# The first token tile in two halves on two DMA queues, with the bias rows moved behind weight tile 4

## The chip, the cores and the metric

The kernel runs on one core of one Trainium2 chip. The metric is device microseconds (us) of one execution. Five engines matter here: TensorE (PE in the profile; its weight loads are PEld), VectorE (DVE), ScalarE (ACT), GpSimd (POOL) and SyncE (SP). SP and ScalarE issue the DMA transfers; 16 DMA engines move the bytes. In the profile, SPq and ACTq are the issuing instructions of SP and ScalarE. Queue q1 carries what SP issues; q10 carries what ScalarE issues (its 0.33 MB are w1's first columns, b1 and one later store of 256 KB).

## What is computed

x is [2048 tokens, 512 features], bf16. Two branches are mixed by a gate per token:

```python
g = sigmoid((x * gate_w).sum(-1, keepdims=True))
a = A_ref(x, wqkv, wo)          # linear attention, 32 heads of 16
h = layernorm(x)                # over the features of a token
u = gelu(einsum("bsd,sf->bdf", h, w1) + b1)     # mixes over the tokens, F = 1792
b = transpose(einsum("bdf,fs->bds", u, w2) + b2)
out = g * a + (1 - g) * b
```

What the change touches is the start of the second branch: the layer norm of x, and the product of w1 [2048 tokens, 1792] with it, which sums over the tokens.

## The kernel before

The tokens come in 16 tiles of 128 (`NT`), one token in each partition. x tile t is `xr[:, t, :]` (128 KB), its normalised form `xh[:, t, :]`. The rows of w1 that belong to token tile t are tile t of w1. Its first 1024 columns (`FA`, eight blocks of 128) are in `w1A[:, t, :]` (256 KB), the rest in `w1B`, loaded later.

**Order of the loads.** Every DMA is issued by the helper `load` (the issue is line 124), by SP unless ScalarE is named, and `pin` keeps the order in which the program lists the instructions on an engine. ScalarE issues three loads first: the 14 rows of b1 into `b_rows` (line 134, 3.5 KB), then the first 128 columns of w1's tiles 0 and 1 (lines 135 and 136, 32 KB each). Then it loads its table and takes a dummy square root (line 137). SP issues x tile 0 (line 139), x tile 1, the other 896 columns of w1's tile 0 (line 141, 224 KB), and then, from line 142 on, one tile of x and one of w1 in turn; of w1's tile 1 it loads the other 896 columns (line 146). Behind w1's tile 4, it loads the 16 rows of b2 into `b_rows` (line 150). Behind the last tile come gate_w, wk, x transposed, and the other weights. `b_rows` is set to zero by VectorE first (line 114), and the loads into it wait for that. Up to eight transfers are under way at a time: each issue waits until the transfer eight earlier in the common list of SP and ScalarE has landed.

**Layer norm.** VectorE takes the statistics of a tile (`ln_bn`, line 197; tile 0, and 4 and up, in one instruction, tiles 1 to 3 in two of 256 features), combines them (`ln_aggr`, line 200), ScalarE takes the square root (`sd`, line 202), and VectorE the reciprocal (line 208) and the normalised tile (`ln_apply`, line 210). The first half of tile t's statistics stands ahead of the normalisation of tile t-1 on VectorE. At t = 8 VectorE turns `b_rows` into columns (line 232).

**First product.** TensorE starts with 18 matmuls on a constant (`warm_ps`). Then, for each of the first 12 token tiles, it does eight matmuls (`accA`, all issued by the helper in line 74), one for each block of 128 columns of w1A: weights w1A, moving operand xh (128x512). The last four tiles go block by block, and each finished block goes to ScalarE (`gelu`). The keys (`kacc`), `Gps`, the other blocks (`accB`), the queries (`qacc`) and the second product (`yps`) follow. The only waits between the loads and TensorE's first matmuls are thus: x tile 0 to xh tile 0, w1's 128 columns for the first weights, w1's other 896 columns for the next seven, and so on for tile 1.

Of the kernel before, what the change touches and what calls it, by code (L numbers as in the profile page):

```python
# [15 lines left out]
def kernel(  # L16
# [13 lines left out]
    nc = tc.nc  # L30
    P = nc.NUM_PARTITIONS
# [11 lines left out]
    NF = F // P  # L43
# [7 lines left out]
    x_view = X.rearrange("(t p) d -> p t d", p=P)  # L51
# [4 lines left out]
    b1_view = B_b1.rearrange("(f p) -> f p", p=P)  # L56
# [9 lines left out]
    def ptile(shape, dt, name):  # L66
        return persist.tile(shape, dt, name=name, tag=name)
# [9 lines left out]
    xr = ptile([P, NT, D], BF16, "xr")  # L77
# [17 lines left out]
    b_rows = ptile([32, P], BF16, "b_rows")  # L95
# [27 lines left out]
    def load(o, i, eng=None, **kw):  # L123
        pin((eng or nc.sync).dma_start(out=o, in_=i, **kw))  # L124

    def load_x(t0, t1):
        load(xr[:, t0:t1, :], x_view[:, t0:t1, :])

    def load_w1a(t):
        load(w1A[:, t, :], w1_view[:, t, 0:FA])  # L130


    tbl = work.tile([P, 1], FP32, name="tbl", tag="tbl", bufs=2)
    load(b_rows[0:NF, :], b1_view, nc.scalar)
    load(w1A[:, 0, 0:P], w1_view[:, 0, 0:P], nc.scalar)
    load(w1A[:, 1, 0:P], w1_view[:, 1, 0:P], nc.scalar)
    pin(nc.scalar.activation(out=tbl[:], in_=eps_t[:], func=ACT.Sqrt))

    load_x(0, 1)
    load_x(1, 2)  # L140
    load(w1A[:, 0, P:FA], w1_view[:, 0, P:FA])
    for t in range(1, NT):
        if t + 1 < NT:
            load_x(t + 1, t + 2)
        if t == 1:
            load(w1A[:, 1, P:FA], w1_view[:, 1, P:FA])
        else:
            load_w1a(t)
        if t == 4:
            load(b_rows[NF : NF + NT, :], b2_view)  # L150
    load(gw_b[:], gw_row_view.to_broadcast([P, D]))
    load(wk_sb[:], wqkv_view[:, :, D : 2 * D])
# [440 lines left out]
```

## Time and profile before

| what | value |
|---|---|
| median of 3 runs | 162.82 us (162.81 to 162.83) |
| span of the profiled execution, first to last instruction | 161.6 us |
| median less span | 1.2 us |
| TensorE busy | 157.1 us, 97% of the span |
| VectorE / ScalarE busy | 118.7 us (73%) / 53.0 us (33%) |
| mean granted TensorE clock | 0.998 |
| bytes moved | 28.33 MB, 175 GB/s over the span |

The profile shows one execution. A line of a timeline begins with the start and the duration in us; at its end, in brackets, stand the engine's idle time before it and what ended that. In tables of issues the last number is the time from an issue's start to its landing, so that issue plus that time is when the data is there. The profiled execution has no time of its own beside its span; the runs without a profile are 1.2 us above it.

### The profile page before, as it was taken

To read this page: it belongs to the slowest core of one execution; us is meant where nothing else is said; L and a number is where in the kernel's file an instruction comes from. 1 tells how busy PE (TensorE), PEld (TensorE's weight loads), DVE (VectorE), ACT (ScalarE), POOL (GpSimd) and SP (SyncE) were. 2 spreads that over 40 slices of the span, in tenths; PEclk is the share of its full clock that TensorE was granted. 3 is DMA by queue.
4 is the path that set the end of the run, shared out by engine and by line. 5 is a ranking of instruction groups with operands and counts; after the bars stand their busy time and mean duration, and the time that the engine had idled before them with its cause. 6 is when DMAs were issued, how large, how long until landed. Compare 5 with 4: busy or idle time off the path is not lost.

```text
span 161.6 us, 2275 instructions
## 1 busy us (share of the span) xinstructions
PE 157.1 (97%) x820; PEld 72.9 (45%) x820; DVE 118.7 (73%) x279; ACT 53.0 (33%) x89; POOL 1.2 (1%) x8
## 2 busy tenths in 40 slices
PE   7899999999999999999999999999999999999993
PEld 5344444444444444444444444444444444444452
DVE  2799998959998998799895999999999980000002
ACT  3122226895243221435225970000008300550050
POOL 2000000000000000000000000000000000000000
PEclk9999999999999999999999999999999999999999
DMA  4999998444699540229953007826535925824421
GB/s 140 271 320 353 364 300 144 101 103 106 159 394 390 149 129 0 87 50 310 402 200 67 0 32 230 322 65 143 186 89 136 353 70 143 265 63 105 143 97 32
DMA packets 36966, 28.33 MB, mean 175 GB/s; under 512 B 20572, under 2 KB 31452, under 8 KB 36956
## 3 DMA queue, kind: packets, MB, share of 16 engines
q1 hardware_dynamic: 36368, 27.87, 57.0%
q10 hardware_dynamic: 588, 0.33, 0.7%
q8 instruction: 6, 0.10, 0.3%
q14 instruction: 4, 0.03, 0.1%
HBM read 19.28 MB, written 4.46 MB: 147 GB/s over the span
## 4 chain that ended last, share of the span: by engine, by line
PE 94%; DMA 3%; SPq 1%; DVE 0%; issue 0%; DVEq 0%
PE yps L74 39%; PE accA L74 16%; PE accB L74 13%; PE qacc L74 9%; PE Gps L74 9%; PE kacc L74 9%; DMA w1A<-in_B_w_dram 3%; SPq L124 1%; PE kvps L74 0%; DVE ot L537 0%; PE w2ps L74 0%; DVEq L537 0%
## 5 line engine op out<-in xcount | busy, mean ns | idle before, releaser
L74 PE MATMUL yps<-uT,w2h 128*128 128x512 bf16 (+2 forms) x238 | 49.2, 366 | 0.0
L74 PEld LDWEIGHTS <-w2h 128*128 128x128 bf16 x238 | 22.8, 98 | 25.9
L74 PE MATMUL accA<-xh,w1A 128*128 128x512 bf16 x128 | 28.0, 379 | 0.8 <-DVE xh L210 0.5
L530 ACT ACTIVATE ot<-yps,c,c 128x512 bf16<-128x512 f32 x15 | 11.6, 777 | 46.9 <-PE yps L74 35.5
L74 PE MATMUL accB<-xh,w1B 128*128 128x512 bf16 x96 | 21.5, 379 | 0.0
L537 DVE TENSOR_SCALAR ot<-yps,c,c 128x384 bf16<-128x384 f32 (+1 forms) x2 | 1.1, 545 | 25.5 <-PE yps L74 25.5
L74 PEld LDWEIGHTS <-w1A 128*128 128x128 bf16 x128 | 12.5, 98 | 16.1 <-DMA w1A<-in_B_w_dram 1.4
L74 PEld LDWEIGHTS <-xT 128*128 128x128 bf16 x128 | 12.4, 98 | 14.9 <-issue 0.2
L74 PE MATMUL kacc<-wk_sb,xT 128*128 128x512 bf16 x64 | 15.8, 379 | 0.0
L74 PE MATMUL Gps<-pk,xr 128*128 128x512 bf16 x64 | 15.8, 379 | 0.0
L74 PE MATMUL yps<-W2sb,pqT 128*128 128x512 bf16 (+2 forms) x68 | 14.6, 366 | 0.0
L74 PEld LDWEIGHTS <-w1B 128*128 128x128 bf16 x96 | 9.4, 98 | 11.3
L74 PE MATMUL qacc<-wq_sb,xT 128*128 128x512 bf16 x64 | 14.5, 379 | 0.0
L286 ACT ACTIVATE e<-qacc 128x512 bf16<-128x512 f32 x16 | 9.6, 597 | 12.2 <-DVE kvbdT L434 4.6
L286 ACT ACTIVATE e<-kacc 128x512 bf16<-128x512 f32 x16 | 9.2, 598 | 12.7 <-DVE pk L293 6.8
L197 DVE BATCH_NORM_STATS2 stats<-xr 128x6 f32<-128x512 bf16 (+1 forms) x19 | 11.1, 586 | 2.7 <-DMA xr<-in_A_x_dram 2.7
L288 DVE TENSOR_SCALAR e<-e 128x512 bf16<-128x512 bf16 x32 | 9.2, 288 | 4.6 <-ACT e L286 4.3
L406 DVE SCALAR_TENSOR_TENSOR pq<-pq,odds,rd 128x512 bf16<-128x512 bf16 x16 | 12.0, 752 | 0.6
L402 DVE TENSOR_REDUCE den<-prod 128x32 f32<-128x544 f32 x16 | 11.5, 720 | 0.6
L293 DVE SCALAR_TENSOR_TENSOR pk<-kacc,e 128x512 bf16<-128x512 f32 x16 | 11.1, 692 | 1.0
L293 DVE SCALAR_TENSOR_TENSOR pq<-qacc,e 128x512 bf16<-128x512 f32 x16 | 11.1, 692 | 0.6
L245 DVE CUSTOM_DVE_ANT_0 junk<-xr,gw_b 128x512 bf16<-128x512 bf16 x16 | 11.0, 689 | 0.4
(52 smaller groups left out, 95.0 us busy)
## 6 DMA issues: line engine op xcount, KB each, us to landing
w2h<-in_B_w_dram SPq DMA_DIRECT2D x3, 1792.0 KB, 7.5
w1A<-in_B_w_dram SPq DMA_DIRECT2D x14, 256.0 KB, 4.7
w1B<-in_B_w_dram SPq DMA_DIRECT2D x4, 768.0 KB, 6.2
xr<-in_A_x_dram SPq DMA_DIRECT2D x16, 128.0 KB, 4.1
q_dram<-pq SPq DMA_DIRECT2D x16, 128.0 KB, 3.7
out_dram<-ot SPq DMA_DIRECT2D x15, 128.0 KB, 1.8
w2h<-in_B_w_dram SPq DMA_DIRECT2D x1, 1280.0 KB, 6.5
wk_sb<-in_A_wqkv_dram SPq DMA_DIRECT2D x1, 512.0 KB, 6.5
```

The costliest lines, as they stand in the source:

```text
L74: nc.tensor.matmul(o, lhsT=lhsT, rhs=rhs, start=start, stop=stop, **kw)
L124: pin((eng or nc.sync).dma_start(out=o, in_=i, **kw))
L197: pin(nc.vector.bn_stats(out=stats[t][:, h, :], in_=xr[:, t, d0:d1]))
L245: nc.vector.tensor_tensor_reduce(out=junk[:], in0=xr[:, t, :], in1=gw_b[:], scale=1.0, scalar=0.0, op0=ALU.mult, op1=ALU.add, accum_out=gp ...
L286: pin(nc.scalar.activation(out=e[:], in_=acc[:], func=ACT.Exp))
L288: nc.vector.tensor_scalar(out=e[:], in0=e[:], scalar1=1.0, scalar2=PHI_EPS, op0=ALU.min, op1=ALU.add)
L293: nc.vector.scalar_tensor_tensor(out=o, in0=acc[:], scalar=0.0, in1=e[:], op0=ALU.max, op1=ALU.add)
L402: pin(nc.vector.tensor_reduce(out=den[:], in_=prod[:], op=ALU.add, axis=AX.X))
L406: nc.vector.scalar_tensor_tensor(out=heads, in0=heads, scalar=odds[:, t : t + 1], in1=rd[:].unsqueeze(2).to_broadcast([P, NH, HEAD]), op0= ...
L530: nc.scalar.activation(out=ot[:, d0:d1], in_=yps[:, d0:d1], func=ACT.Identity, scale=c1[:, t : t + 1], bias=c2[:, t : t + 1],)
L537: nc.vector.tensor_scalar(out=ot[:, d0:d1], in0=yps[:, d0:d1], scalar1=c1[:, t : t + 1], scalar2=c2[:, t : t + 1], op0=ALU.mult, op1=ALU.add,)
```

## The change

x tile 0 is loaded in two halves of 64 tokens (64 KB each): tokens 64 to 127 on ScalarE's queue, as its first instruction, in the place of b1's rows; tokens 0 to 63 on SP's, in the place of the whole tile. w1's first 128 columns of tiles 0 and 1 stay behind it on ScalarE's queue. b1's 14 rows are now issued by SP, behind w1's tile 4 and ahead of b2's rows. SP has one issue more than before, ScalarE as many as before. The instructions of TensorE, VectorE and GpSimd and their order are the same; the statistics of tile 0 wait for two transfers instead of one, and the turning of `b_rows` waits for two.

```diff
     tbl = work.tile([P, 1], FP32, name="tbl", tag="tbl", bufs=2)
-    load(b_rows[0:NF, :], b1_view, nc.scalar)
+    HP = P // 2
+    load(xr[HP:P, 0, :], x_view[HP:P, 0, :], nc.scalar)
     load(w1A[:, 0, 0:P], w1_view[:, 0, 0:P], nc.scalar)
     load(w1A[:, 1, 0:P], w1_view[:, 1, 0:P], nc.scalar)
     pin(nc.scalar.activation(out=tbl[:], in_=eps_t[:], func=ACT.Sqrt))
 
-    load_x(0, 1)
+    load(xr[0:HP, 0, :], x_view[0:HP, 0, :])
     load_x(1, 2)
     load(w1A[:, 0, P:FA], w1_view[:, 0, P:FA])
     for t in range(1, NT):
...
         if t == 4:
+            load(b_rows[0:NF, :], b1_view)
             load(b_rows[NF : NF + NT, :], b2_view)
```

## Prediction

> **What bounds the kernel now.** I read the chain that ended last first, on the page:
>
> ```profile
> PE yps L74 39%; PE accA L74 16%; PE accB L74 13%; PE qacc L74 9%; PE Gps L74 9%; PE kacc L74 9%; DMA w1A<-in_B_w_dram 3%; SPq L124 1%; PE kvps L74 0%; DVE ot L537 0%; PE w2ps L74 0%; DVEq L537 0%
> ```
>
> TensorE makes up 94% of it, and the only transfer in it is of w1A, with 3%. The same view, cut to the first 25 us and in order of time, says where:
>
> ```profile
> 2.20 0.43 SPq L124
> 2.63 0.04 issue
> 2.67 4.65 DMA w1A<-in_B_w_dram
> 7.32 0.04 issue
> 7.37 17.66 PE accA L74 x81
> ```
>
> From 7.37 us TensorE runs without a break (81 matmuls in 17.66 us, 218 ns each). What starts that run is the SP transfer issued at 2.67, the last 896 columns of w1's tile 1; I call it W1 (and W0 the same part of tile 0). The waits of TensorE over the whole run agree: no wait for an input of over 0.1 us stands behind 7.37 except one of 0.4 for DVE, in its weight loads, which run ahead of the matmuls. So the change, which ends within the first loads, can move the end only as far as it moves 7.37. The timeline of the first 8 us shows what lies ahead of it:
>
> ```profile
> 0.80 0.87 SPq L124 DMA_DIRECT2D xr<-in_A_x_dram  x2
> ...
> 0.87 0.11 DVE L114 MEMSET b_rows<- 32x64 uint32 x1 [0.87 <-PEq L577]
> ...
> 1.02 0.63 ACTq L124 DMA_DIRECT2D b_rows<-in_B_b_dram  x1
> ...
> 1.68 0.86 ACTq L124 DMA_DIRECT2D w1A<-in_B_w_dram  x2
> ...
> 2.58 1.28 ACT L137 ACT_TABLE_LOAD   x1 [2.58 <-issue]
> ...
> 2.92 0.69 DVE L197 BATCH_NORM_STATS2 stats<-xr 128x6 f32<-128x512 bf16 x1 [1.93 <-DMA xr<-in_A_x_dram]
> ...
> 4.95 2.10 PE L74 MATMUL accA<-xh,w1A 128*128 128x512 bf16 x9 [0.50 <-DVE xh L210]
> ...
> 7.37 6.87 PE L74 MATMUL accA<-xh,w1A 128*128 128x512 bf16 x31 [0.31 <-DMA w1A<-in_B_w_dram]
> ```
>
> The reader should see two gaps of TensorE: 0.50 us before its first matmul on data, at 4.95, and 0.31 us before 7.37. The first nine matmuls (eight of token tile 0, one of tile 1) stand between them. **The second gap swallows the first**: if the nine start earlier and W1 lands as now, the second gap only grows. The issue table cut to each issue gives landings: x tile 0 at 0.80 + 2.1 = 2.90, tile 1 at 3.36, w1's first 128 columns of tile 0 at 1.68 + 3.1 = 4.78, W0 at 1.72 + 3.3 = 5.02, x tile 2 at 5.4, W1 at 2.67 + 4.7 = 7.37, x tile 3 at 3.15 + 4.6 = 7.75. Engine use by stretch (columns: window, its length, busy time and count of five engines, granted clock, DMA share, GB/s):
>
> ```profile
> 1.80:2.20 0.40, 0.40 (x4) 0.28 (x2) 0.00 (x0) 0.00 (x0) 0.05 (x1) 1.00 0.66 159
> 2.20:2.60 0.40, 0.40 (x4) 0.28 (x3) 0.00 (x0) 0.03 (x1) 0.00 (x0) 1.00 0.95 309
> ...
> 4.40:5.60 1.20, 0.70 (x5) 0.39 (x4) 1.13 (x5) 0.09 (x1) 0.00 (x0) 1.00 0.83 142
> 5.60:7.00 1.40, 1.40 (x7) 0.49 (x5) 1.33 (x5) 0.21 (x1) 0.00 (x0) 1.00 0.91 291
> ```
>
> The DMA engines start slowly (159 GB/s), then 309, and sag to 142 GB/s while W1 is due. W1 is no matter of its issue: it waits behind 608 KB on SP's queue.
>
> **The change part by part.**
>
> *ScalarE's queue.* b1's 14 rows leave it (1.02 to 1.65, after DVE's memset of b_rows that ended at 0.98), and x's lower 64 tokens come instead, with no wait: start 0.80 like SP's, for 0.40 (SP's first issue) to 0.63 (the row it replaces). The two w1 issues then start at 1.25 to 1.48 instead of 1.68, the Sqrt table load at 2.15 to 2.38 instead of 2.58. I take 0.3 earlier. So w1's 128 columns land at about 4.5 (4.78 now).
>
> *x tile 0.* Each half is 64 KB. How long a half takes isn't in the trace; the nearest rows are the stores at the kernel's end, 128 KB in 1.8 us and 32 KB in 1.4, which give 0.27 us for 64 KB. Bounds: the halves land 0.27 earlier, or, if ScalarE's issue needs 0.63 and its half lands no sooner after it, 0.23 later. I take 0.2 earlier. The statistics need both halves. Further, sd started at 3.98 though its input ended at 3.65 + 0.18 = 3.83, because the table load and the dummy Sqrt ran until then; that 0.12 goes as well (a usual gap there is 0.03). First matmul: 4.95 - 0.2 - 0.12 = 4.63. By itself this is **worth nothing at the end**: the nine matmuls need 9 x 0.22 = 2.0 us and would wait at 6.6 instead of 7.05 for W1 at 7.37.
>
> *SP's queue ahead of W1.* Its number of issues is the same and an issue takes 0.40 to 0.43 whatever its size here (16 rows of b2 took 0.36), so W1 is issued at most 0.05 earlier. But 64 KB less lie ahead of W1 on that queue. Between x tile 0's landing (2.90) and W1's (7.37), it delivered tile 1, W0, tile 2 and W1, 704 KB in 4.47 us: 6.35 ns a KB, so 64 KB are 0.41 us. At the pace of the window 7 to 8 us (370 GB/s) they would be 0.18. They must go by the other queue, though. Room for them is in the slow start: 159 GB/s against 309 in the next 0.4 us is 60 KB not moved, just as ScalarE's half is due: SP's first bytes move at 1.8, 1.0 us behind its first issue, and ScalarE's half is issued as early. I take 0.4 for that reason, as W1's lateness was built up in the slow stretches, and keep 0 and 0.77 as ends. 0.77 is what remains if W1 stops mattering: matmuls that run on from 4.63 reach the tenth at 6.6.
>
> *What is late next.* Tile 2's normalised tokens (DVE, 8.28 + 0.41 = 8.69) are needed at 7.37 + 7 x 0.218 = 8.90: only 0.21 to spare. They wait for x tile 3 (DVE takes tile 3's first half before it finishes tile 2), which lands at 7.75 right behind W1 on the same queue. If W1 comes earlier, tile 3 should; if it doesn't, the gain ends at 0.21. Each later tile is needed 8 x 0.218 = 1.74 later: tile 3 has 10.64 - 10.34 = 0.30 to spare, tile 4 0.87, tile 6 2.0.
>
> *b1 on SP's queue behind tile 4.* One more issue of 0.36, and one more place in the row of eight transfers that may be under way: tile 6 of x was released at 7.34 by W1's landing; now b2 takes that place and tile 6 waits for tile 3's landing, 7.75. The transfers behind come about 0.5 later. Cover: x tile 6 lands at 10.7, then 11.2, and its statistics start at 11.53; w1's tile 5 lands at 7.75 + 3.9 = 11.65, then 12.2, and is needed at 14.13. Without that cover it would cost 0.5. The bias transposes on DVE wait for b1 and b2 at 15.1, long after. Cost: nothing. DVE and TensorE instructions are the same, in the same order.
>
> **Sum.** The profiled execution spans 161.6 us; the median of the runs is 162.82, so about 1.2 lie outside the span, which the change doesn't touch. 161.6 - 0.4 = 161.2, or **162.42** by the median.
>
> The Trainium skill speaks against the change (DMA: Bandwidth & Descriptors, "Issuing engines are not separate DMA queues"): transfers started by SP and ScalarE run on the same 16 DMA engines and interleave, and a second issuing engine saves only issue time. By that rule 64 KB moved to the other queue delay W1 as before, and the time stays at about 162.8. The trace agrees in that both queues move packets in the same stretch (2.6 to 5 us: SP's take 85.4% of the 16 engines' time, ScalarE's 12.6%); that the start leaves 60 KB of room is why I don't follow it all the way.
>
> **The rivals.**
> 1. *Hidden anyway.* The DMA engines are the limit, not the queue, and W1 lands at 7.37 within 0.2. For: 0.82 to 0.95 busy from 2.2 on, and the same bytes in all. Against: the weak start. Time 162.8. (This is where the rule just named leads.)
> 2. *Tile 3 becomes the limit.* W1 lands 0.4 earlier, x tile 3 doesn't, and TensorE stops at token tile 2. Gain 0.21: 162.61. For: slack of only 0.21. Against: both are on one queue.
> 3. *Slower: ScalarE's queue pushes W1 back.* It now has 128 KB instead of 67, and 64 KB of it come ahead of w1's columns; served in turn with SP's, they reach into the stretch of 142 GB/s, where 64 KB cost 0.46: 163.28. It decides once W1 lands later than 7.70. For: that stretch is there and not explained by bytes. Against: ScalarE's issues start earlier.
>
> **How the numbers follow.** 0.2% is 0.33 us, about what a measurement of this kernel can tell from no change. Forecast (gain of 0.33 to 0.77): 0.45. Rival 2: 0.12, rival 1: 0.21, both within 0.2%: 0.33. Rival 3: 0.22. The range goes from the full 0.77 (162.05; rounded to 162.1) to rival 3 (163.28; rounded to 163.2): about 0.02 and 0.1 lie outside.
>
> **What would show it.** W1's landing near 6.97 and the unbroken run from there; first matmul at 4.6 to 4.7 with the gap before the run still open; statistics of tile 0 at 2.7; the table load near 2.3; x tile 6 issued behind tile 3's landing, without a wait on TensorE. I am wrong if W1 still lands at 7.3 or later, if tile 2's normalised tokens end last, or if any wait of TensorE appears behind 9 us.

## The result and the profile after

The changed kernel is slower: ratio 1.0036 to the kernel before, 95% interval 1.0023 to 1.0049, or about 0.6 us. Its median is 163.62 us (163.16 to 164.82, 13 runs) beside 162.87 (162.8 to 163.56, 13 runs) on the same chip. The prediction was 162.42, a gain of 0.4.

The profiled executions tell less than the runs: spans of 161.8 and 161.6. Each later run came with its span, and time less span is 1.7 to 1.8 us throughout, for both kernels, so the 161.6 of the first page belongs to an execution of about 163.3 us, not to the median of 162.82. A second profile of the kernel before has 161.4. Single executions of one kernel spread by about 1 us here, and the traces below show what varies; verdicts rest on ratios of many runs. A run more than 1.5% above the fastest of its kernel is left out of a ratio, which here is one run alone, of 165.82 us.

The chain of the page after:

```profile
PE yps L74 38%; PE accA L74 17%; PE accB L74 13%; PE kacc L74 9%; PE qacc L74 9%; PE Gps L74 8%; DMA xr<-in_A_x_dram 2%; DVE stats L199 0%; PE kvps L74 0%; DVE xh L212 0%; DVE ot L539 0%; PE w2ps L74 0%; ACT sd L204 0%; DVE mv L202 0%; DVE rstd L210 0%
```

The one transfer in the chain is now of x, not of w1A. In order of time, the first 9 us of the chain (start, length, what):

```profile
0.80 2.45 DMA xr<-in_A_x_dram
...
3.35 0.70 DVE stats L199
...
4.82 0.42 DVE xh L212
5.24 0.04 issue
5.28 3.82 PE accA L74 x16
```

x tile 0 lands at 3.25 (2.90 before), and the end is followed back through its layer norm and the first matmul, 5.28 (4.95 before). The timeline shows what was slow ahead of it:

```profile
0.80 1.45 SPq L124 DMA_DIRECT2D xr<-in_A_x_dram  x2
0.80 0.55 ACTq L124 DMA_DIRECT2D xr<-in_A_x_dram  x1
...
1.39 1.07 ACTq L124 DMA_DIRECT2D w1A<-in_B_w_dram  x2
...
2.31 0.41 SPq L124 DMA_DIRECT2D w1A<-in_B_w_dram  x1
2.49 1.28 ACT L138 ACT_TABLE_LOAD   x1 [2.49 <-issue]
...
3.35 0.69 DVE L199 BATCH_NORM_STATS2 stats<-xr 128x6 f32<-128x512 bf16 x1 [2.35 <-DMA xr<-in_A_x_dram]
...
5.28 9.08 PE L74 MATMUL accA<-xh,w1A 128*128 128x512 bf16 x39 [0.45 <-DVE xh L212]
```

SP's first two issues took 1.45 us, 0.57 for the half and 0.82 for x tile 1 behind it (0.87 for both before), and ScalarE's half 0.55. W0 is issued at 2.31 instead of 1.72, W1 at 3.24 instead of 2.67. Three things could do that: two engines issuing at the same moment, the 64 rows, or the split itself; and b1's new place could cost elsewhere.

### The profile page after: what moved, and what is told of

It is laid out like the page before. It is cut to its first block, busy times and chain, and to the rows that moved or that the text cites. A ratio compares the mean times of both kernels' runs of the same rounds, so it can differ in the third digit from the quotient of the medians.

```text
span 161.8 us, 2264 instructions
## 1 busy us (share of the span) xinstructions
PE 156.9 (97%) x806; PEld 73.0 (45%) x820; DVE 119.0 (74%) x279; ACT 53.1 (33%) x89; POOL 1.2 (1%) x8
## 4 chain that ended last, share of the span: by engine, by line
PE 94%; DMA 2%; DVE 1%; issue 1%; ACT 0%; DVEq 0%
PE yps L74 38%; PE accA L74 17%; PE accB L74 13%; PE kacc L74 9%; PE qacc L74 9%; PE Gps L74 8%; DMA xr<-in_A_x_dram 2%; DVE stats L199 0%; PE kvps L74 0%; DVE xh L212 0%; DVE ot L539 0%; PE w2ps L74 0%; ACT sd L204 0%; DVE mv L202 0%; DVE rstd L210 0%
```

## The experiments

All were timed against the kernel before in five rounds. The first four shared its 29 runs (median 163.16), the next four 31 others (162.97), the last four 35 others (162.97).

**e0, the kernel before again.** No edit.

> The kernel before against itself: ratio 1.000 within 0.1%. It shows what its runs' spans are beside their times: the changed kernel's runs have 1.75 us around the span, the profiled execution of before 1.2. If the runs of before have 1.75 too, the 0.5 us is no cost of the change, and its spans should be near 161.1; if they have 1.2, half a microsecond of the change's cost lies outside the span.

Measured: 1.0002 [0.9989, 1.0016], median 163.14, spans 1.7 to 1.8 below the times. So none of the change's cost lies outside the span.

**e1, b1 alone moved.**

```diff
-    load(b_rows[0:NF, :], b1_view, nc.scalar)
...
         if t == 4:
+            load(b_rows[0:NF, :], b1_view)
```

> Only b1 moves behind w1's tile 4 on SP's queue; x tile 0 is whole, on SP's. ScalarE now issues w1's first columns at 0.80, at the same moment as SP issues x tile 0. Theory A (two issues at the same moment hold each other up): SP's first two issues take 0.55 to 0.8 us each instead of 0.40, x tile 0 lands at 3.2 instead of 2.90, first matmul at 5.2 to 5.3 instead of 4.95, time up by 0.3 to 0.6 us. Theory B (two halves on two queues are what costs): time as before, first matmul 4.9 or earlier. Theory C (b1's place on SP's queue costs): up by 0.5 us or so, with x tile 6 late and first matmul as before.

Measured: 0.9998 [0.9984, 1.0012]. Both engines issue at 0.80, SP for 0.40 and 0.42, ScalarE for 0.40 and 0.47: the clash is no cause, theory A falls, and theory C with the time. Theory B is left, though not in its first matmul: x tile 0 landed 0.2 later (3.09), while ScalarE's columns, issued at 0.80 as well, were under way, and the first matmul came at 5.05.

**e2, the halves alone.** b1 stays on ScalarE's queue, behind w1's columns.

```diff
     load(w1A[:, 1, 0:P], w1_view[:, 1, 0:P], nc.scalar)
+    load(b_rows[0:NF, :], b1_view, nc.scalar)
...
-            load(b_rows[0:NF, :], b1_view)
```

> Only x tile 0 in two halves on two queues; b1's rows stay on ScalarE's queue, as its last load. Theory A: both engines issue at 0.80, first issues 0.55 each, first matmul near 5.28, time up by 0.6 us as in the changed kernel. Theory B: the same time, but with first issues of 0.40. Theory C: time as before or faster.

Measured: 1.0063 [1.0033, 1.0093], issues of 0.57 and 0.55 again, with nothing of b1 on SP's queue. First matmul in its profile 5.57. Two things meet there: x tile 1, issued behind the half for 0.83, landed only at 4.49, and b1's issue on ScalarE's queue stands ahead of the table load, which began at 3.19 instead of 2.49, so that the square root of tile 0 waited until 4.60 for it. So e2 isn't the halves and nothing else. Its times are mostly 163.6 to 163.8, but four of twelve lie between 164.4 and 165.8. The profile is one of those (columns: window, length, busy time and count by engine, clock, DMA share, GB/s):

```profile
5.60:9.00 3.40, 3.40 (x9) 1.17 (x9) 2.82 (x11) 0.59 (x2) 0.00 (x0) 1.00 0.92 288
9.00:12.40 3.40, 3.40 (x17) 1.55 (x16) 3.29 (x12) 0.89 (x3) 0.00 (x0) 1.00 1.04 374
```

Nine matmuls in 3.4 us, then seventeen, with no wait between them: TensorE ran at half clock until 9.0. (The clock column reads 1.00 even so; it seems to count only from the first record of the granted clock on, which the trace of this run has at 9.03. Where the clock "came up" below, the time is that of this first record.)

**e3, both halves on SP's queue.**

```diff
-    load(xr[HP:P, 0, :], x_view[HP:P, 0, :], nc.scalar)
...
     load(xr[0:HP, 0, :], x_view[0:HP, 0, :])
+    load(xr[HP:P, 0, :], x_view[HP:P, 0, :])
```

> x tile 0 in two halves, both on SP's queue; ScalarE's queue has w1's first columns alone, from 0.80; b1 on SP's. Theory A: the clash at 0.80 is there as well, and one more issue (0.4 us) stands ahead of x tile 1: up by 0.6 to 1.0 us. Theory B: no more than the issue of 0.4 us, hidden in part: 0 to 0.4 us. Theory C: 0.5 us as in e1.

Measured: 1.0121 [1.0085, 1.0158], more than any of the theories said. Issues of 0.57, 0.57, and 0.58 for the whole tile 1 behind them, while ScalarE's beside them took 0.39 and 0.46: the slow issue goes with the 64 rows, on one queue or two. First matmul 5.79, half clock until 10.21.

**e4, halves by features.** 128 rows of 256 features (`HC` is 256), the same bytes on the same queues.

```diff
-    load(xr[HP:P, 0, :], x_view[HP:P, 0, :], nc.scalar)
+    load(xr[:, 0, HC:D], x_view[:, 0, HC:D], nc.scalar)
...
-    load(xr[0:HP, 0, :], x_view[0:HP, 0, :])
+    load(xr[:, 0, 0:HC], x_view[:, 0, 0:HC])
```

> The changed kernel, but x tile 0 is halved by features (128 rows of 256) instead of by tokens (64 rows of 512); same bytes, same queues, b1 behind tile 4. Theory D (a transfer of 64 rows takes long to issue, 0.57 us, and so does the one behind it): the issues take 0.40 to 0.45 us, W0 is issued at 1.7 again, x tile 0 lands at 2.9 or sooner, first matmul at 4.7 to 4.95, time 0 to 0.3 us below before. Rival E (two halves on two queues cost by themselves, since both must land): x tile 0 at 3.2, first matmul 5.2, up 0.5 us as in the changed kernel.

Measured: 1.0016 [1.0, 1.0031]. Timeline:

```profile
0.80 0.40 SPq L124 DMA_DIRECT2D xr<-in_A_x_dram  x1
...
0.80 0.41 ACTq L124 DMA_DIRECT2D xr<-in_A_x_dram  x1
...
1.26 0.41 SPq L124 DMA_DIRECT2D xr<-in_A_x_dram  x1
...
2.98 0.69 DVE L199 BATCH_NORM_STATS2 stats<-xr 128x6 f32<-128x512 bf16 x1 [1.99 <-DMA xr<-in_A_x_dram]
```

The slow issues are gone, the first matmul is at 4.92. But two queues bring nothing either: the halves land at 2.8 and 3.0, not ahead of the whole tile's 2.90. Still 0.2 us were left over, which theory D didn't expect.

**e5, 20 matmuls on the constant instead of 18**, in the changed kernel.

```diff
-    for _ in range(18):
+    for _ in range(20):
```

> The changed kernel with 20 instead of 18 matmuls on the constant, so that TensorE is busy until 5.27 at half clock and the gap of 0.45 us before the first matmul closes. Theory D with the clock (the later first matmul leaves a longer gap, and in some runs the granted clock comes up a window later): the runs of 164 and more go, median 0.1 to 0.4 us below the changed kernel. Without the clock: median as the changed kernel's, 0.4 to 0.6 us above before.

Measured: 1.0048 [1.0031, 1.0065], median 163.77, and three of the eight runs at 164.0 to 164.3. Neither a lower median nor an end to the runs of 164 and more: a miss for theory D as I put it. None reached the 164.8 of the changed kernel's longest, but eight runs don't settle that. The gap was closed (first matmul 5.27, right behind the constant ones), and its profile still ran at half clock until 6.45.

**e6, 96 tokens on SP's queue, 32 on ScalarE's.**

```diff
-    HP = P // 2
+    HP = 3 * P // 4
```

> The changed kernel with 96 tokens of tile 0 on SP's queue and 32 on ScalarE's. Theory D in its narrow form (64 rows alone are slow): both first issues take 0.32 to 0.45 us, W0 is issued at 1.7, first matmul at 4.95 or sooner, time within 0.1 us of before or below it. In its wide form (any load of fewer than 128 rows of x): 0.55 us or more, first matmul at 5.2 to 5.3, up 0.5 us.

Measured: 1.0025 [1.0012, 1.0039]. The issues took 0.41 and 0.42: of x loads of 32, 64, 96 and 128 rows in this place, those of 64 alone are slow. (Not of all loads: b1's 14 rows of 256 bytes took 0.63 on ScalarE's queue in the kernel before, and 0.38 on SP's in the changed one.) x tile 0 landed at 3.04 all the same, its statistics began at 3.14 and the first matmul came at 5.10, so the narrow form of D is right on the issues and wrong on the time.

**e7, x tile 1 ahead of tile 0**, in the kernel before.

```diff
-    load_x(0, 1)
     load_x(1, 2)
+    load_x(0, 1)
```

> The kernel before with x tile 1 issued ahead of x tile 0 on SP's queue, both whole. x tile 0 is issued at 1.26 instead of 0.80, and nothing of the 64 rows is in it. Theory D (lateness of x tile 0 is what costs, through the first matmul and the clock): first matmul at 5.4, up 0.4 to 0.6 us in the fastest runs, with some runs 2 us above. Rival F (W1's landing at 7.3 sets the time, as the prediction had it): the nine matmuls end at 7.4, time up by 0 to 0.1 us.

Measured: 1.0026 [1.0009, 1.0042], the longest run 164.21, none 2 us above. Tile 0 came even later than expected:

```profile
1.26 2.71 DMA xr<-in_A_x_dram
...
5.94 6.85 PE accA L74 x31
```

First matmul at 5.94, 1.0 us later than before, for 0.4 us of time. So lateness of tile 0 does cost, but less than one for one: the first product's matmuls, which then waited for nothing, took 0.3 to 0.5 us less than in the two profiles of the kernel before.

**e8, the kernel before with one transfer more**, wv in two loads.

```diff
-    load(wv_sb[:], wqkv_view[:, :, 2 * D : 3 * D])
+    load(wv_sb[:, 0:2, :], wqkv_view[:, 0:2, 2 * D : 3 * D])
+    load(wv_sb[:, 2:ND, :], wqkv_view[:, 2:ND, 2 * D : 3 * D])
```

> The kernel before with wv loaded in two halves, far from the start and from any wait of TensorE, so that the program has one transfer more, as the changed kernel has. Theory G (at the end SP waits for the last transfer of each of its places one after the other; one transfer more moves the last store from the last place to an earlier one, and two short waits then follow it): span less the start of the last VectorE instruction 2.84 instead of 2.72 us, time up by 0.12 us, the first 25 us as before. Rival (the end differs by chance, or through the load of b1): 2.72, ratio 1.000.

Measured: 1.0014 [0.9997, 1.0031]; from the start of the last VectorE instruction to the end of the span 2.84 us instead of 2.72. The profile shows something else besides. Its first loads are those of the kernel before, yet W1 (issued at 2.67 as there) landed at 6.70, and the chain to the unbroken run goes through w1's first columns on ScalarE's queue:

```profile
1.68 3.42 DMA w1A<-in_B_w_dram
5.09 0.05 issue
5.14 6.87 PE accA L74 x31
```

The second gap, the wait for W1 on which the prediction rests, isn't there.

**e9, the changed kernel with one transfer less**, w1B in three loads.

```diff
-    for t0 in range(0, NT, 4):
-        load(w1B[:, t0 : t0 + 4, :], w1_view[:, t0 : t0 + 4, FA:F])
+    for t0, t1 in ((0, 8), (8, 12), (12, NT)):
+        load(w1B[:, t0:t1, :], w1_view[:, t0:t1, FA:F])
```

> The changed kernel with w1B in three loads instead of four, so that the number of transfers is that of before. Theory G: the end is 2.72 us again, 0.12 us less than the changed kernel's run beside it; the first 8 us unchanged (issues of 0.57, first matmul near 5.28), so still 0.2 to 0.4 us above before. Rival: all of the cost lies in the first 8 us, nothing changes.

Measured: 1.0025 [1.0001, 1.0048], median 163.24, fastest 163.02; the end is 2.72 us again, the issues are 0.57 as before. One of its eleven runs is of 165.28, and much of the 1.0025 hangs on it: the mean of the other ten is 0.08% above that of the kernel before's 35 runs.

**e10, the changed kernel again.** No edit.

> The changed kernel once more, beside e8, e9 and e11 on the same chip: 0.3 to 0.5% above before; its fastest runs 0.35 us above the fastest of before, of which 0.12 lie at the end; a profile with the granted clock coming up at another time than 5.49.

Measured: 1.0034 [1.0021, 1.0048], median 163.65, fastest 163.14 against 162.78. TensorE in its profile:

```profile
0.84 4.00 PE L74 MATMUL warm_ps<-const-bfloat16-1.0 128*128 128x256 bf16 x18 [0.84 <-PEq L579]
5.23 7.00 PE L74 MATMUL accA<-xh,w1A 128*128 128x512 bf16 x30 [0.39 <-DVE xh L212]
```

The 18 constant matmuls took 4.00 us, at half clock throughout (3.62 in the first profile of before, where the clock came up at 3.9); it came up at 5.99. From 5.23 on TensorE waits for nothing, W1 included.

**e11, halves by features and one transfer less.** The edits of e4 and e9 together.

> Column halves (as in the run with 128 rows of 256 features) and w1B in three loads: neither the slow issue nor the longer end. Theory D with G: time as before within 0.1 us, fastest runs 162.8 to 162.9; the split itself brings nothing, since x tile 0 lands at 2.96 against 2.90. The prediction's relief of W1 would make it 0.3 us or more faster than before.

Measured: 1.0004 [0.9989, 1.002], median 163.22, fastest 162.73. With both causes taken away the time is that of before, and the interval lies below the changed kernel's (1.0023 to 1.0049). Nothing here beats the kernel before. The first matmul came at 5.05 although x tile 0 had landed at 2.92, because VectorE takes the first half of tile 1's statistics first, and x tile 1 landed at 4.04 (3.34 before).

**Two causes.** Ratios by form of the first loads and by number of transfers:

| first loads | transfers as before | one more |
|---|---|---|
| 128 rows | e0 1.0002, e1 0.9998, e11 1.0004 | e4 1.0016, e8 1.0014 |
| two halves of 64 rows | e9 1.0025 | changed 1.0036, e10 1.0034 |

In the right column two halves of 64 rows cost about 0.2% (0.3 us); e6, with 96 and 32 rows and one transfer more, stands between with 1.0025. In the left one that isn't shown: without its one long run e9 has nearly the mean of e11 (0.08 us more), and the medians are the same, 163.24 and 163.22; only the fastest runs differ, 163.02 against 162.73. The transfer more goes with 0.1% (0.1 to 0.2 us) in the upper row; the lower one hangs on e9 again. Single intervals are as wide as these steps. What the times show by themselves is that both together make up the loss (e11 against the changed kernel).

The traces show both mechanisms in every profile. Issues took 0.55 to 0.58 wherever one of the first loads had 64 rows. The first matmul came at 4.92 to 5.14 in the seven profiles without such a load (e7 left aside), at 5.17 to 5.28 in four with it (changed, e5, e9, e10), and at 5.57 and 5.79 in e2 and e3. The end took 2.71 to 2.73 us in all profiles with the old number of transfers (before, e0, e1, e7, e9, e11) and 2.83 to 2.85 in all with one more (changed, e2 to e6, e8, e10). At the end SP waits for the last transfer of each place in turn, in five waits. Before, the wait for the last store was the fifth; with one transfer more it stands third of five in the trace, and two short waits of 0.06 us each follow it. Between the first product and the end nothing costs anything: from the start of the last matmul of the first product to the end of the span it is 128.72 to 128.74 us in all profiles with the old number, and 128.84 to 128.86 in all with one more but e5, whose TensorE waited 0.27 us for a load of w2 at 130 us. So apart from the 0.12, all that the profiles differ by lies ahead of the end of the first product, at 33 us.

## Why the prediction was wrong

The sum had one term, 0.4 us from W1 landing earlier. That term failed: it measured nothing. e11 has halves on two queues without the two costs found here, and its ratio is 1.0004 [0.9989, 1.002], where 0.4 us less would be 0.9975, outside the interval. In its place stand two costs that the prediction had put at nothing, the slow issue of 64 rows (about 0.3 us where the runs show it) and one transfer more among the waits at the end (0.12 us). Step by step:

- **An issue takes 0.40 to 0.43 whatever its size here.** This is the first step that failed in order of time. I took b2's 16 rows as proof, though the trace of before has loads of 64 rows, of wo:

```profile
49.05 0.56 SPq L124 DMA_DIRECT2D wo_sb<-in_A_wo_dram  x1
49.66 0.58 SPq L124 DMA_DIRECT2D wo_sb<-in_A_wo_dram  x1
...
53.20 0.32 SPq L124 DMA_DIRECT2D wo_sb<-in_A_wo_dram  x1
```

  The first two have 64 rows, the third 96. The nearest row to a load of 64 rows of 1 KB was there, and it was right to 0.02. It was no sure price, though: among the same loads of wo, one of 32 rows took 1.20 us to issue and another of 32 rows 0.32, one of 96 rows 0.44, and two stores of 128 rows late in the kernel took 0.58. What no row showed is that the issue behind it on its queue takes 0.57 to 0.86 as well.
- **ScalarE's queue 0.3 earlier.** 1.39 instead of 1.25 to 1.48 for w1's first columns was inside the bounds; the second pair of issues was slow too, so the table load began at 2.49, 0.1 earlier.
- **x tile 0 lands 0.2 earlier.** It landed 0.35 later, beyond the bound of 0.23. Even without the slow issue, 64 KB each on two queues gained nothing (e4: 2.96, e11: 2.92). The estimate let the time shrink with the bytes, as it does for the stores at the end. At the start it hardly does: of loads issued at 0.80, 32 KB landed at 2.87 (e6), 64 KB at 2.79 and 2.96 (e4), the whole 128 KB at 2.90 (before).
- **64 KB less ahead of W1 are worth 0.4.** With W1 issued at 2.67 as before and these 64 KB on the other queue, it landed at 7.16 (e4) and 7.55 (e11), against 7.32, 7.13 and 6.70 in three profiles with the first loads of before (before, e0, e8). No gain shows against a spread of 0.6 us that I had no idea of from one profile; rival 1 was right on this. The changed kernel's W1 landed at 7.37, the sign that I had named for being wrong, although it was issued 0.57 later. So its issue wasn't what held it, as I had said.
- **Worth nothing at the end: the second gap swallows the first.** That holds only where W1 lands after the first nine matmuls have ended, which two things decide that I had read off one profile. W1's landing is one: issued at 2.66 or 2.67, it landed anywhere from 6.43 (e1) to 7.55 (e11). The clock is the other: where it comes up at 5.5 to 6, the first nine matmuls take longer. A second gap of over 0.1 us stands in three of the fourteen profiles (before 0.31, e0 0.12, e11 0.44). Without it a later first matmul counts. I had taken the clock of one profile, up at 3.92, as the rule; in eleven of the thirteen other traces it came up anywhere from 3.8 to 6.5, and in two at 9.0 and 10.2 (e2, e3). The Trainium skill has this (TensorE: Matmul & The Clock Gate, Part 1: The HAM clock gate): a window of about 3.4 us that runs freely decides on the clock, so that the ramp differs from run to run. The traces agree: the record of the full clock lasts 157.01 us in twelve of them and 153.60, just 3.41 less, in e2 and e3.
- **Long runs, which I hadn't foreseen.** Of 62 runs of kernels with 64-row loads at the start, 11 are above 164.3; of 192 others, 120 of them of the kernel before, none is. The profiles of e2 (165.27) and e3 (165.93) are of such runs, and there the full clock came up late; the three single ones (164.8 to 165.8, one each of the changed kernel, e9 and e10) fit that, though none of them was profiled. That the idle time ahead of the first matmul is the cause (0.73 us in e2, 0.95 in e3, both while the clock was still half) isn't shown: e7 had 1.31 us there, behind a clock up at 4.26, and no long run in twelve.
- **b1 costs nothing.** Right: e1 0.9998, though x tile 6 did wait for tile 3, as foreseen (7.83).
- **Not seen: one transfer more at the end,** 0.12 us. I counted the instructions of the change up to the last load and not the waits behind the last store.
- The rival on the slower side named the right sign and nearly the size (0.46), but W1 was not pushed back (7.37 against 7.32). The mechanism was another, so its number came near by luck.

Open: why 64 rows take longer than 32, 96 or 128; what the 64 rows cost where there is no transfer more (e9); what makes the clock come up late in some runs; and how the 0.3 us divide between the later first matmul and the later loads behind it. e5 didn't separate them.

## What to carry to other kernels

Price a changed transfer by rows of the same number of partitions as well as of the same bytes, and look at how far such rows spread. Where TensorE's first work falls into its warm-up, one profile shows one phase of the clock and one landing of each load; take a second profile before calling an edit hidden behind a wait. And a transfer added anywhere can move the last store in the row of waits at the end.

## What the runs showed of the hardware

- A load of 64 rows of 1 KB took 0.55 to 0.58 us to issue on SP's and ScalarE's queue, the next issue on that queue 0.57 to 0.86; loads of x of 32, 96 and 128 rows took 0.40 to 0.42 in the same place.
- Two engines that issued at the same moment didn't hold each other up (e1: 0.40 and 0.40).
- At the start a load's size hardly showed in its landing: 32, 64 and 128 KB issued at 0.80 landed 2.0 to 2.2 us later (e6, e4, before).
- The same load, issued at the same time (W1, at 2.66 or 2.67 in eight profiles), landed between 6.43 and 7.55.
- The full clock came between 3.8 and 10.2 us after the start. The kernel before, whose first matmuls fall into that time, spread from 162.78 to 164.0 from run to run.
- One transfer more in the program lengthened the end, from the last VectorE instruction on, from 2.72 to 2.84 us.
